# Batch 1's frequency products in three instead of four: a spectral filter with a feed-forward layer on one Trainium2 core

## The chip, the core and the metric

The kernel runs on one core of one Trainium2 chip. A core has TensorE (PE in the profile, its weight loads PEld), VectorE (DVE), ScalarE (ACT), GpSimd (POOL) and SyncE (SP), which issues most DMAs. Each engine takes its own instructions in order. TensorE writes to PSUM, eight banks of 2 KB for each of the 128 partitions; VectorE and ScalarE read PSUM, GpSimd works in SBUF only. The metric is the device time of one execution in microseconds (us).

## What is computed

```python
X = np.fft.rfft(x, axis=1)                      # x: 8 batches, 3008 rows, 256 columns
Yr = Xr @ w_r - Xi @ w_i + b_r
Yi = Xr @ w_i + Xi @ w_r + b_i
Yr = sign(Yr) * max(abs(Yr) - 0.01, 0); the same for Yi
y = np.fft.irfft(Yr + 1j * Yi, n=3008, axis=1)
h = y @ moe_w_in                                # 256 -> 2048
g = where(h > 0, h, exp(min(h, 0)) - 1)
out = g @ moe_w_out                             # 2048 -> 256
```

The kernel does the two Fourier transforms as matrix products in two stages each (3008 = 47 x 64).

## The kernel before, in words

**The main loop** (line 1207) has 47 steps for each batch (`PER`), 376 in all. Step i computes a pair of 128-wide slices of h for a block of 512 rows (`front`, L986, four products 128x512 at L1006 into the tile hps), the exponential on ScalarE (L1022 to L1027), the finish of the step before on VectorE (`finish_elu`, L1048 or L1050, hps and Et to gT), and the second layer's products of step i-2 (`back`, L1080, into ps_o). From step 10 on hps has two buffers, so the hps of step i take the buffer of step i-2, which is free when that step's L1048 or L1050 has run. Every eighth step ends a block, and ps_o is copied out (L1092).

**Between these**, the spectral filter of the next batch is put into the steps as units: A (first transform stage, of the batch after next), X (`unit_X`, L194, its second stage, eight units into the tile XT), M (`unit_M`, L264, the products with the weights, twelve units (q, i), 128 frequencies each), B (`unit_B`, L364, the first inverse stage, six units; B(v) needs both M(v, 0) and M(v, 1)), and Y (`unit_Y`, L530). The function `plan` (L1110) writes out, for each batch, which unit goes into which step: list f0 holds what is issued ahead of `front`, f1 what comes after `finish_elu`. For batch 0's steps, in which batch 1's units run, the order starts at step 10 (`lead = FILL`): X in steps 10 to 17, M(0,0), M(0,1), M(1,0), M(1,1), B(0) in 18 to 22, then M, M, B in turn: B(1) in step 25, B(2) in 28, B(3) in 31, then M(5,0), M(5,1), B(4), B(5) in 32 to 35, and A units and the first Y units from step 36. Steps 0 to 9 hold batch 1's A units and batch 0's last Y units (`split_Y`).

**Who computes the negative branch** changes with the step. In an M step (`on_act`) ScalarE does two passes (L1024, L1025). In steps 0 to 9, and in the later batches' "pool" steps, GpSimd clamps Et (L1059). In the remaining steps that hold a unit, batch 0's X, B and A steps among them, VectorE does it (L1061, one operation of 128x1024 ahead of L1050).

**M units.** A frequency's product of complex X with complex W can be had from four real products (Xr Wr, Xi Wi, Xr Wi, Xi Wr) or from three, with (Xr + Xi) Wr shared and the weight sums Wi + Wr and Wi - Wr. Batches 2 to 7 use three: six products of 128x256 (L289) into two PSUM tiles, of which VectorE copies one (k1) to SBUF (L295, shown as L144) and adds it to the other (L296); GpSimd adds the bias (L301), clips (L302) and subtracts (L303). Their inputs Xr + Xi come from `sum_XT` (L219, GpSimd, L224, six sums of 128x512 a batch, five into XS and one into the tile busy), and the weight sums from `three_weights` (L232, GpSimd, L236, four operations in place on wcat_s, steps 47 to 50). Batches 0 and 1 use four: `m_group` (L240) issues four products of 128x512 (L247), VectorE adds the bias on the way out of PSUM (L257), GpSimd clips and subtracts (L269, L270).

**X units.** Unit u of batches 2 to 7 takes the eight slots of group u % 4 and the half u // 4 of the 256 columns d. Batch 0's and batch 1's take group u // 2 and half u % 2, so that a group of slots is used up before the next. The slots come from the tile Z, which `load_Z` reads back from DRAM; for batch 1 in three parts (slots 0 to 7, 8 to 15, 16 to 31), issued on SyncE's queue in step 5. In step 12 GpSimd runs `gate` (L860), a small copy that waits for Z's third part, ahead of the load of batch 2's first x tile (`load_x`, L117, issued on GpSimd's queue in steps 12, 15 and 18).

Of the kernel before, what the change touches and what calls it, by code (L numbers as in the profile page):

```python
# [8 lines left out]
ALU = mybir.AluOpType  # L9
# [20 lines left out]
def kernel(  # L30
# [11 lines left out]
    nc = tc.nc  # L42
    P = nc.NUM_PARTITIONS

    B, S, D = x.shape
# [5 lines left out]
    LAM = 0.01  # L51
# [42 lines left out]
    PER = S * NPAIR // TB  # L94
# [9 lines left out]
    Y_of = {}  # L104
# [14 lines left out]
    def unit_ps(name, alone):  # L119
        if alone:  # L120
            return pre2.tile([P, 2, 512], F32, name=name, tag="pre2")
        return last_banks("psF").tile([P, 2, 512], F32, name=name, tag="fps")
# [69 lines left out]
        q.dma_start(Z_of[b][r0:r1, s0:s1, :], dv[r0:r1, s0:s1, :])  # L192

    def unit_X(b, u, alone=False, on_dve=False, apart=False):  # L194
        g, dt = (u % 4, u // 4) if b > 1 else (u // 2, u % 2)
        if u == 0:
            XT_of[b] = xtp.tile([P, 2, 2, K1 * N2], BF16, name="XT", tag="XT")
        XT, Z = XT_of[b], Z_of[b]
        if apart:
            psv = [t[:].rearrange("p (k j) -> p k j", j=P) for t in two_banks(pre1, "mps1")]  # L200
        else:
            ps = unit_ps("xps", alone)
            psv = [ps[:].rearrange("p a (k j) -> p (a k) j", j=P)]
        nk = 8 // len(psv)
        for kk in range(8):
            k = 8 * g + kk
            nc.tensor.matmul(  # L207
                psv[kk // nk][:, kk % nk, 0 : 4 * K1], lhsT=Z[:, k, dt * P : dt * P + P],
                rhs=M2[:, k].rearrange("p c m -> p (c m)"), start=True, stop=True,
            )  # L210
        for h, v in enumerate(psv):
            k0 = 8 * g + nk * h
            evac(
                XT[:, dt].rearrange("p c (m s) -> p c m s", s=NS)[:, :, :, k0 : k0 + nk],
                v[:, :, 0 : 4 * K1].rearrange("p k (c m) -> p c m k", c=2),
                bool(h) if apart else on_dve,
            )
# [14 lines left out]
    def three_weights(c, dt):  # L232

        v, r = (w[:, dt, D * c : D * c + D] for w in (wcat_s, wcat_r))
        a, b_ = (r, v) if c else (v, r)
        nc.gpsimd.tensor_tensor(v, a, b_, ALU.subtract)  # L236

    mps_of = {}

    def m_group(b, q, i, ps, biased=False):  # L240
        XT = XT_of[b]
        o = (2 * q + i) * P
        todo = [(c, dt) for c in range(2) for dt in range(2)]
        if b == 0:
            todo.sort(key=lambda z: z[1])
        for c, dt in todo:
            nc.tensor.matmul(  # L247
                ps, lhsT=XT[:, dt, c, o : o + P], rhs=(wcat_r, wcat_s)[c][:, dt, :],
                start=(not biased and (c, dt) == (0, 0)), stop=((c, dt) == (1, 1)),
            )  # L250
        if i == 0:
            Y_of[b, q] = wk3.tile([P, 2, 2 * D], BF16, name="Y", tag="Y")
        if biased:
            yb = ps
        else:
            yb = wk3.tile([P, 2 * D], F32, name="yb", tag="yb")[:]
            nc.vector.tensor_tensor(yb, ps, bias_bc[:], ALU.add)  # L257
        if (b, q, i) == (0, 2, 0):
            clip = late3.tile([P, 2 * D], F32, name="gT", tag="gT")
        else:  # L260
            clip = wk2.tile([P, 2 * D], F32, name="clip", tag="clip")
        return yb, clip

    def unit_M(b, q, i):  # L264
        if b == 1:
            if i == 0:
                mps_of[q] = unit_ps("mps", False)
            yb, clip = m_group(b, q, i, mps_of[q][:, i, :])
            nc.gpsimd.tensor_scalar(clip[:], yb, LAM, -LAM, ALU.min, ALU.max)  # L269
            nc.gpsimd.tensor_tensor(Y_of[b, q][:, i, :], yb, clip[:], ALU.subtract)  # L270
            return
        XT, o = XT_of[b], (2 * q + i) * P
        if i == 0:
            Y_of[b, q] = wk3.tile([P, 2, 2 * D], BF16, name="Y", tag="Y")
        ps, k1 = (
            last_banks("psM").tile([P, 2 * D], F32, name="mps", tag="mps") for _ in range(2)
        )
        ch, oc = divmod(o, 512)
        r, s = wcat_r, wcat_s
        todo = [  # L280
            (k1[:, 0:D], None, r[:, :, 0:D]),
            (ps[:, 0:D], XT[:, :, 1, o : o + P], s[:, :, 0:D]),
            (ps[:, D : 2 * D], XT[:, :, 0, o : o + P], s[:, :, D : 2 * D]),
        ]
        if o == 0 and b > 3:
            todo.append(todo.pop(0))
        for out_, lhs, w in todo:
            for dt in range(2):
                nc.tensor.matmul(  # L289
                    out_, lhsT=lhs[:, dt] if lhs is not None else sum_of(dt, ch)[:, oc : oc + P],  # L290
                    rhs=w[:, dt, :], start=(dt == 0), stop=(dt == 1),
                )
        yb = wk3.tile([P, 2 * D], F32, name="yb", tag="yb")
        clip = wk2.tile([P, 2 * D], F32, name="clip", tag="clip")
        evac(yb[:, D : 2 * D], k1[:, 0:D], True)  # L295
        nc.vector.tensor_tensor(  # L296
            yb[:].rearrange("p (c d) -> p c d", c=2),
            ps[:].rearrange("p (c d) -> p c d", c=2),
            yb[:, D : 2 * D].unsqueeze(1).to_broadcast([P, 2, D]), ALU.add,
        )  # L300
        nc.gpsimd.tensor_tensor(yb[:], yb[:], bias_bc[:], ALU.add)  # L301
        nc.gpsimd.tensor_scalar(clip[:], yb[:], LAM, -LAM, ALU.min, ALU.max)  # L302
        nc.gpsimd.tensor_tensor(Y_of[b, q][:, i, :], yb[:], clip[:], ALU.subtract)  # L303
# [107 lines left out]
    def two_banks(pool, n):  # L411
        return [pool.tile([P, 512], F32, name=n, tag=n) for _ in range(2)]
# [697 lines left out]
    def plan(b):  # L1110

        f0 = [[] for _ in range(PER)]
        f1 = [[] for _ in range(PER)]
        mode = [None] * PER
        n1, n2 = b + 1, b + 2
# [6 lines left out]
        if n1 < B:  # L1122
            if b:
                lead, xs = 0, (3, 6, 9) if b < 3 else (3, 8, 13)
# [28 lines left out]
        else:  # L1153
            lead, seq = 0, [("y", u) for u in range(2, 8)]
# [39 lines left out]
        if n2 < B:  # L1194
            for ci in range(3):
                f1[xs[ci]].append((load_x, (n2, ci)))
        if b and n1 < B:
            f0[seq.index(("X", 4))].append((sum_XT, (n1, 0)))
            f0[seq.index(("X", 7))].append((sum_XT, (n1, 1, range(2 if b < 3 else 3))))
            if b < 3:  # L1200
                f0[seq.index(("M", 2, 0))].insert(0, (sum_XT, (n1, 1, (2,))))
        return f0, f1, mode

    f0 = f1 = None
    bare = 0
    early_h = None
    for i in range(n + LAG):
        if i == FILL:
            few.close()
            psH = ctx.enter_context(  # L1210
                tc.tile_pool(
                    name="psH", bufs=2, space=bass.MemoryType.PSUM, reuse_waits="tile"
                )
            )
        if i == LAG:
            back(0, False)
        if early_h:
            h, on_act = early_h, False
        elif i < n:
            r = i % PER  # L1220
            if r == 0:
                f0, f1, mode = plan(i // PER)
                used = [bool(u0 or u1) for u0, u1 in zip(f0, f1)]
            free = not used[r]
            bare = bare + 1 if free else 0
            calm = free and (i >= n - 2 or (r + 2 < PER and not used[r + 1] and not used[r + 2]))
            for f, a in f0[r]:
                f(*a)
            if mode[r]:
                on_act = mode[r] == "act"  # L1230
                pooled = not on_act
            else:
                on_act = any(f is unit_M for f, a in f0[r])
                pooled = free or i < FILL
            third = calm and bare % 3 == (2 if i // PER == B - 1 else 1)
            h = front(i, third, on_act, pooled)
        finish_elu()
        if i < n:
            for f, a in f1[r]:
                f(*a)  # L1240
            split = i > LAG and (i - LAG) % NPAIR == NPAIR - 1
            if split:
                back(i - LAG, True)
            elu(i, *h, pooled, on_act)
            if PER <= i < PER + 4:
                three_weights(*divmod(i - PER, 2))
            if 1 <= i < 5:
                if i < 3:
                    scale_w_in(2, True, i - 1)
                scale_w_in(3, False, (i - 1) // 2, (i - 1) % 2)  # L1250
            if i == n - 2:
                early_h = front(n - 1, True, False, True)
            elif early_h:
                early_h = None
        else:
            split = False
        if i > LAG and not split:
            back(i - LAG, False)
# [30 lines left out]
```

## Time and profile before

| | |
|---|---|
| device time, median of 3 runs | 894.43 us (894.23 to 895.2) |
| span of the profiled execution | 903.9 us, 18292 instructions |
| TensorE busy | 891.3 us, 99% of the span |
| VectorE, ScalarE, GpSimd busy | 679.6, 722.4 and 596.7 us |
| TensorE's granted clock | 0.948 on average |
| steps 10 to 17 (batch 1's X) | 73.4 to 90.9 us of the span |
| steps 18 to 35 (batch 1's M and B) | 90.9 to 139.0 us |
| GpSimd busy from 90.9 to 136.7 us | 23.22 of 45.8 us |

Times in a trace are us from the start of the span, durations in us or ns. The profile gives no time of the profiled execution other than its span, which is longer than the runs without a profile. In a timeline, matmuls that follow one another overlap, since their ends are modelled: the start of a group is what counts. The chain of work that ended last shows each group only for the time in which nothing before it on the chain was running. Brackets at the end of a timeline's line give how long the engine sat idle before it and what ended that.

### The profile page before, as it was taken

What the parts mean: (1) busy time and instruction counts of PE and PEld (TensorE: products, weight loads), DVE (VectorE), ACT (ScalarE), POOL (GpSimd) and SP (SyncE); (2) the same over time, 40 slices, a digit from 0 to 9 for tenths busy, and PEclk for the clock granted to TensorE, in tenths of its full rate; (3) what the DMA queues carried; (4) which work ended last, traced back from release to release, by engine and by line L of the source; (5) the groups of instructions that cost most, each with busy time, mean ns of one, the idle gap of its engine ahead of it and who ended that gap; (6) DMA issues with size and microseconds to landing.
All of it is one profiled execution on the core that took longest, in us unless ns stands there. A gap on an engine that the chain in (4) does not pass through costs nothing.

```text
span 903.9 us, 18292 instructions
## 1 busy us (share of the span) xinstructions
PE 891.3 (99%) x6917; PEld 675.2 (75%) x6917; DVE 679.6 (75%) x969; ACT 722.4 (80%) x1001; POOL 596.7 (66%) x806
## 2 busy tenths in 40 slices
PE   9999999999999999999999999999999999999997
PEld 3467667877788777877778777787777877777776
DVE  7788778688866887668866788677876678778776
ACT  6778778888978889798887988878887798776654
POOL 7562550788657886588756877559875697753664
PEclk9999999999999999999999999999999999999998
DMA  8996226631474115632265231643218201241111
GB/s 262 310 258 188 70 71 181 169 119 47 118 209 124 65 50 152 173 117 88 72 181 136 86 116 48 189 140 101 87 53 229 70 24 48 69 108 36 28 44 47
DMA packets 90718, 105.85 MB, mean 117 GB/s; under 512 B 5395, under 2 KB 81174, under 8 KB 87302
## 3 DMA queue, kind: packets, MB, share of 16 engines
q1 hardware_dynamic: 84278, 76.64, 30.0%
q0 software_dynamic: 5968, 27.26, 9.4%
q8 instruction: 54, 0.88, 0.4%
q10 hardware_dynamic: 384, 0.79, 0.3%
q14 instruction: 34, 0.28, 0.1%
HBM read 54.86 MB, written 49.81 MB: 116 GB/s over the span
## 4 chain that ended last, share of the span: by engine, by line
PE 90%; DVE 3%; DMA 3%; ACT 2%; POOL 1%; issue 1%; SPq 0%; DVEq 0%; ACTq 0%; POOLq 0%
PE ps_o L1080 37%; PE hps L1006 36%; PE mps L289 5%; PE bps L375 2%; PE xps L207 2%; PE yps L538 2%; PE aps L170 2%; DVE gT L1048 2%; PE mps L247 1%; DVE Bz L144 1%; DMA xt<-in_x_dram 1%; DMA Z<-DA 1%; DMA DB<-Bz 1%; PE sps L1006 1%; DMA DA<-A 0%
## 5 line engine op out<-in xcount | busy, mean ns | idle before, releaser
L1048 DVE SCALAR_TENSOR_TENSOR gT<-Et,hps 128x512 fp32r<-128x512 f32 (+1 forms) x544 | 423.7, 811 | 158.5 <-POOL Et L1059 115.4
L1080 PE MATMUL ps_o<-w_out_r,gT 128*128 128x256 f32 x3008 | 481.4, 303 | 0.0
L1080 PEld LDWEIGHTS ps_o<-w_out_r,gT 128*128 128x128 f32 x3008 | 407.7, 190 | 52.4 <-ACT osb L1092 0.5
L1059 POOL TENSOR_SCALAR Et<-Et 128x512 f32<-128x512 f32 x434 | 258.3, 614 | 223.6 <-ACT Et L1022 213.2
L1006 PE MATMUL hps<-yT,w_in_s 128*128 128x512 bf16 (+7 forms) x1688 | 388.9, 360 | 2.0 <-DVE gT L1048 1.3
L1022 ACT ACTIVATE Et<-hps 128x512 f32<-128x512 f32 x412 | 224.2, 598 | 67.8 <-PE hps L1006 63.3
L1006 PEld LDWEIGHTS <-w_in_s 128*128 128x128 bf16 x1728 | 144.7, 99 | 119.7 <-issue 21.7
L1024 ACT ACTIVATE Et<-hps 128x1024 f32<-128x1024 f32 x130 | 133.6, 1027 | 57.3 <-PE hps L1006 49.0
L1025 ACT ACTIVATE Et<-Et 128x1024 f32<-128x1024 f32 x130 | 137.4, 1057 | 4.1
L301 POOL TENSOR_TENSOR yb<-yb,bias_bc 128x512 f32<-128x512 f32 x72 | 92.3, 1282 | 9.5 <-DVE yb L296 9.4
L303 POOL TENSOR_TENSOR Y<-yb,clip 128x512 bf16<-128x512 f32 x72 | 92.6, 1286 | 6.0
L296 DVE TENSOR_TENSOR yb<-mps,yb 128x512 f32<-128x512 f32 x72 | 49.8, 692 | 7.6 <-PE hps L1006 0.5
L146 ACT CAST XT<-xps 128x768 bf16<-128x768 f32 x57 | 45.5, 799 | 9.8 <-PE xps L207 9.7
L146 ACT CAST A<-aps 128x1024 bf16<-128x1024 f32 x40 | 40.5, 1014 | 11.4 <-PE aps L170 9.9
L302 POOL TENSOR_SCALAR clip<-yb 128x512 f32<-128x512 f32 x72 | 44.2, 614 | 6.3
L289 PE MATMUL mps<-wcat_s,XT 128*128 128x256 bf16 x288 | 44.1, 277 | 0.0
L144 DVE COPY yb<-mps 128x256 f32<-128x256 f32 x72 | 30.3, 421 | 11.1 <-PE mps L289 9.7
L1050 DVE SCALAR_TENSOR_TENSOR gT<-hps,Et 128x1024 fp32r<-128x1024 f32 x29 | 35.5, 1223 | 2.4
L224 POOL TENSOR_TENSOR XS<-XT 128x512 bf16<-128x512 bf16 x30 | 34.1, 1159 | 2.1 <-ACT XT L146 1.2
L1092 DVE COPY osb<-ps_o 128x512 f32<-128x512 f32 x46 | 31.6, 686 | 1.2 <-PE ps_o L1080 0.5
L146 ACT CAST Bz<-bps 128x1024 bf16<-128x1024 f32 x32 | 31.9, 998 | 0.5 <-PE bps L375 0.4
L1027 ACT ACTIVATE Et<-hps 128x1024 f32<-128x1024 f32 x29 | 29.8, 1029 | 2.6 <-PE hps L1006 1.2
(184 smaller groups left out, 678.8 us busy)
## 6 DMA issues: line engine op xcount, KB each, us to landing
xt<-in_x_dram POOLq DMA_DIRECT2D x21, 1024.0 KB, 5.4
out_dram<-osb SPq DMA_DIRECT2D x158, 128.0 KB
Bs<-DB SPq DMA_DIRECT2D x30, 384.0 KB
DB<-Bz SPq DMA_DIRECT2D x20, 512.0 KB
DA<-A SPq DMA_DIRECT2D x19, 512.0 KB
Z<-DA SPq DMA_DIRECT2D x5, 1152.0 KB
Z<-DA SPq DMA_DIRECT2D x11, 384.0 KB
xt<-in_x_dram POOLq DMA_DIRECT2D x6, 512.0 KB, 6.0
```

The lines of the kernel that those rows point to most:

```text
L146: nc.scalar.copy(dst, src)
L289: nc.tensor.matmul(out_, lhsT=lhs[:, dt] if lhs is not None else sum_of(dt, ch)[:, oc : oc + P], rhs=w[:, dt, :], start=(dt == 0), stop=(d ...
L296: nc.vector.tensor_tensor(yb[:].rearrange("p (c d) -> p c d", c=2), ps[:].rearrange("p (c d) -> p c d", c=2), yb[:, D : 2 * D].unsqueeze(1 ...
L301: nc.gpsimd.tensor_tensor(yb[:], yb[:], bias_bc[:], ALU.add)
L303: nc.gpsimd.tensor_tensor(Y_of[b, q][:, i, :], yb[:], clip[:], ALU.subtract)
L1006: nc.tensor.matmul(hps[s][:, c0:c1] if early else hps[:, s, c0:c1], lhsT=w_in_s[:, dt, ft * P : ft * P + P], rhs=yT_of[b][:, dt, t0 : t0 + ...
L1022: nc.scalar.activation(E_[:, s], hps[:, s], AF.Exp)
L1024: nc.scalar.activation(E_, hps[:], AF.Relu, scale=-1.0)
L1025: nc.scalar.activation(E_, E_, AF.Exp, scale=-1.0)
L1048: nc.vector.scalar_tensor_tensor(o, e, -1.0, h, ALU.add, ALU.max)
L1059: nc.gpsimd.tensor_scalar(E_[s], E_[s], 1.0, 0.0, ALU.min, ALU.max)
L1080: nc.tensor.matmul(po[q][:, i_ % 2, :], lhsT=gT[:, s, i_ * P : i_ * P + P], rhs=w_out_r[:, ft, :], start=(ft == 0 and i_ % 2 == 0), stop=( ...
```

## The change

Batch 1's M units lose their own branch and run the code of batches 2 to 7. For this, its X units take the order by halves of d (all four groups for the first half, then all four for the second), `sum_XT` runs on GpSimd after X4's issue in step 14 (first half, three sums) and after X7's in step 17 (second half, three sums), and `three_weights` runs in steps 6 to 9 instead of 47 to 50. M(0,0) of batch 1 issues its product with the sums last of three. Batch 0 keeps four products.

```diff
     def unit_X(b, u, alone=False, on_dve=False, apart=False):
-        g, dt = (u % 4, u // 4) if b > 1 else (u // 2, u % 2)
+        g, dt = (u % 4, u // 4) if b else (u // 2, u % 2)
...
-    mps_of = {}
-
...
     def unit_M(b, q, i):
-        if b == 1:
-            if i == 0:
-                mps_of[q] = unit_ps("mps", False)
-            yb, clip = m_group(b, q, i, mps_of[q][:, i, :])
-            nc.gpsimd.tensor_scalar(clip[:], yb, LAM, -LAM, ALU.min, ALU.max)
-            nc.gpsimd.tensor_tensor(Y_of[b, q][:, i, :], yb, clip[:], ALU.subtract)
-            return
         XT, o = XT_of[b], (2 * q + i) * P
...
-        if o == 0 and b > 3:
+        if o == 0 and (b == 1 or b > 3):
             todo.append(todo.pop(0))
...
-        if b and n1 < B:
+        if b == 0:
+            f0[lead + 4].append((sum_XT, (n1, 0)))
+            f0[lead + 7].append((sum_XT, (n1, 1)))
+        elif n1 < B:
             f0[seq.index(("X", 4))].append((sum_XT, (n1, 0)))
...
-            if PER <= i < PER + 4:
-                three_weights(*divmod(i - PER, 2))
+            if 6 <= i < 10:
+                three_weights(*divmod(i - 6, 2))
```

## Prediction, on record before the result

> **What bounds the kernel now.** I read the page first: engine shares, then the chain of work that ended last.
>
> ```profile
> PE 891.3 (99%) x6917; PEld 675.2 (75%) x6917; DVE 679.6 (75%) x969; ACT 722.4 (80%) x1001; POOL 596.7 (66%) x806
> ...
> PE 90%; DVE 3%; DMA 3%; ACT 2%; POOL 1%; issue 1%; SPq 0%; DVEq 0%; ACTq 0%; POOLq 0%
> ```
>
> TensorE bounds the whole, so a shorter product is worth its full length, unless TensorE then waits. The change acts in two stretches of the timeline: batch 1's X units (steps 10 to 17, from 73.4 us) and its M and B units (steps 18 to 35, 90.9 to 139 us). Next the chain there, and the same work of batch 2 (start, length, what):
>
> ```profile
> 104.54 0.90 PE mps L247 x4
> 105.45 0.90 PE hps L1006 x4
> 106.34 0.94 PE ps_o L1080 x8
> ...
> 187.76 0.68 PE mps L289 x6
> 188.44 0.89 PE hps L1006 x4
> ```
>
> An M step today is 0.90 + 0.90 + 0.94 us with no gap. Batch 2's M unit, which already has three products, takes 0.68 us.
>
> **Gain.** 12 M units x (0.90 - 0.68) = -2.64 us. That is all: it holds only where TensorE does not wait. So I went through what each step of TensorE waits for. hps has two buffers, so the hps products of step i wait until VectorE's L1048/L1050 of step i-2 has read its buffer. The tightest place is a B step followed by two M steps. VectorE's timeline, then TensorE's (start, length):
>
> ```profile
> 105.13 0.70 DVE L1061 TENSOR_SCALAR Et<-Et 128x1024 f32<-128x1024 f32 x1 [0.60 <-ACT Et L1027]
> 105.74 0.69 DVE L257 TENSOR_TENSOR yb<-mps,bias_bc 128x512 f32<-128x512 f32 x1
> 106.34 1.22 DVE L1050 SCALAR_TENSOR_TENSOR gT<-hps,Et 128x1024 fp32r<-128x1024 f32 x1
> ```
> ```profile
> 108.02 1.06 PE L1006 MATMUL hps<-yT,w_in_s 128*128 128x512 bf16 x4
> ```
>
> M(2,0) starts at 104.39. VectorE first finishes step 22's L1061 (it waits for ScalarE's exp, which stands behind two passes of the M step and the eviction L146), then adds the bias for M (L257), then L1050 of step 22, done at 107.56. Step 24's hps start at 108.02: a margin of 0.46 us.
>
> **Cost 1, VectorE's copy (L295).** After the change one more VectorE operation stands in this queue, in front of L1050. Batch 2 shows it:
>
> ```profile
> 188.38 0.41 DVE L144 COPY yb<-mps 128x256 f32<-128x256 f32 x1
> 188.90 0.69 DVE L296 TENSOR_TENSOR yb<-mps,yb 128x512 f32<-128x512 f32 x1
> ```
>
> From copy to add is 0.52 us. L1050 ends 0.52 later, and two shorter M units bring the hps forward by 0.45. So TensorE waits 0.52 + 0.45 - 0.46 = 0.51 us. ScalarE, and with it L1061, keeps its distance to M(2,0), since both hang on the hps two steps earlier. The same sum at the other places (margins from the same two timelines): steps 18/19 margin 0.55, wait 0.42; 26/27, 0.48 and 0.49; 29/30, 0.48 and 0.49; 32/33, 0.49 and 0.48. Five places: +2.39 us. In batch 2 this doesn't occur, because no L1061 runs on VectorE there. I see no reason for less, except that ScalarE's exp came 0.5 us earlier.
>
> **Cost 2, POOL against VectorE.** POOL gets L301 (1.28 us) for each M unit and six sums L224 (1.16 us each); its 1.97 us per unit (L269, L270) become 3.32 (L301 at 189.67 to the next at 192.99). A group of two M and one B step is 7.98 us long (104.39 to 112.36), POOL's part 6.64: it fits, but POOL is then nearly always at work, where it is now idle when L1061 runs. All 29 L1061 take 683 to 697 ns, so that row alone prices a meeting at nothing. But L1061 passes 1024 elements in the time that L257 needs for 512, as L852 does (512 in 0.42), and L852 met POOL early on. VectorE, then POOL:
>
> ```profile
> 42.67 1.01 DVE L852 TENSOR_SCALAR w_in_s<-w_in_f 128x512 bf16<-128x512 f32 x1 [0.40 <-DMA w_in_f<-in_moe_w_in_dram]
> ...
> 52.91 0.42 DVE L852 TENSOR_SCALAR w_in_s<-w_in_f 128x512 bf16<-128x512 f32 x1
> ```
> ```profile
> 42.08 1.32 POOL L332 TENSOR_TENSOR Y<-yb,clip 128x512 bf16<-128x512 f32 x1
> ```
>
> The first ends at 43.68, 0.28 after POOL's operation (43.40). Others end 0.28 after POOL's at 39.05, 42.27 and 54.66. So L1061 will stand until POOL's running operation ends. At a random moment of 3.32 us with pieces of 1.28, 0.61 and 1.28, the rest of a piece is (1.64 + 0.37 + 1.64) / 6.64 = 0.55 us, less some 0.12 of start-up that runs beside it: 0.43. It delays L1050 in front of the same waits, five times: +2.15 us; bounds 0 (POOL between operations) and 5 x 1.14 = 5.7. I take the mean because the phase isn't known.
>
> The Trainium skill, SBUF — State Buffer, Who interferes with whom, says that GpSimd and a VectorE operation in a two-port mode exclude each other for a whole instruction, and that whoever issues first goes first. The four L852 rows agree; by it POOL too would stand behind L1061. By the L1061 row alone the sum below would be 2.55 lower.
>
> **Cost 3, sums in the X steps.** The three sums of the first half (step 14) meet one or two L1061 of X steps. There L1050 ends at 82.31 and the next hps but one starts at 82.51: margin 0.20. A sum of 1.14 leaves 0.57 - 0.14 = 0.43 on average, 0.2 past the margin, twice: +0.4; bounds 0 and 1.6. The second half's first sum starts after X7's eviction (89.27 + 0.80) and ends by 91.3; M(0,0) asks for it last, at 91.4: no wait. L224 in front of load_x delays a load that is used 40 us later: nothing.
>
> **Cost 4, Z earlier.** X2 now reads Z's third part (slots from 16), at step 12 instead of step 14. TensorE's X2 and POOL's gate on that part:
>
> ```profile
> 77.78 0.52 PE L207 MATMUL xps<-M,Z 96*128 96x96 bf16 x8
> ```
> ```profile
> 78.21 0.63 POOL L860 CAST gate<-Z 96x1 f32<-96x1 bf16 x1 [4.81 <-DMA Z<-DA]
> ```
>
> It lands at about 78.2: +0.4 us (bounds 0 and 0.5). X1 reads the second part at 75.59, when about 6 us of transfer since 69.5 have passed for the first half of the bytes: nothing.
>
> **Cost 5, the last B unit.** B(5) needs both M(5) results from POOL. Batch 2's shows the pair's length:
>
> ```profile
> 231.46 1.28 POOL L301 TENSOR_TENSOR yb<-yb,bias_bc 128x512 f32<-128x512 f32 x1 [0.97 <-DVE yb L296]
> ...
> 236.85 1.27 POOL L303 TENSOR_TENSOR Y<-yb,clip 128x512 bf16<-128x512 f32 x1
> ```
>
> 6.66 us. From M(5,0)'s start (128.34 now): L1061 until 1.35 (+0.43), copy 0.52, add 0.69, hand-over 0.1, POOL 6.66: 9.75. TensorE would otherwise reach B(5) at 136.66 - 128.34 = 8.32, less 0.45, plus 0.48 and 0.43 of costs 1 and 2: 8.78. Wait +1.0 us. In batch 2 an A unit stands before B(4), which hides this. B(0) (needed some 10.6 us after M(0,0), POOL done at 9.9 or with the waits both later) and B(1) to B(4): nothing, by a margin that is thin at B(0) only. Steps 35 and 36 lose 0.1 to VectorE's lateness today; after that wait they don't: -0.1.
>
> **Moved to nothing.** The four L236 (0.67 us) go to steps 6 to 9, where POOL sits idle 0.77 and then 1.43 us a step before its clamp L1059; without that cover each would cost TensorE up to 0.67. Out of steps 47 to 50 they free POOL time that TensorE doesn't wait for (its steps there are 2.19 us, without gaps).
>
> **Sum.** -2.64 + 2.39 + 2.15 + 0.4 + 0.4 + 1.0 - 0.1 = +3.6 us. The profiled execution's span is 903.9 us, 1.1% over the runs' median of 894.43; the page gives nothing of what lies around it. The terms are differences inside the span; 1.1% of them is 0.04, so I carry them unscaled: 894.4 + 3.6 = 898.0.
>
> **Rivals.**
> - *No meeting on POOL's side* (costs 2 and 3 vanish): L1061 falls between POOL's operations, or goes first. For it: 29 undisturbed rows. Against it: POOL idle in all of those. 898.0 - 2.55 = 895.5. Chance 0.2.
> - *Faster*: every M unit's 0.22 us is kept, because exp and L1061 come at least 0.5 us earlier beside M (ScalarE catching up while it has less to wait for), so L1050 is in time in spite of the copy, and POOL ends M(5) in time for the same reason. Decides at a margin of 0.97 us in front of hps instead of 0.46. Then -2.64 + 0.4 = 892.2. Against it: ScalarE's two passes start from the hps that shift along. Chance 0.12.
> - *POOL becomes the bound*: every meeting costs nearly a whole operation and POOL, held in turn, delays each B unit. Cost 2 at 5.7, cost 3 at 1.6: 898.0 + 3.55 + 1.2 = 902.8. POOL's 6.64 in 8 us speaks against a lasting queue. Chance 0.08.
> - That the change doesn't do what it says can be excluded nearly: the products follow from the code.
>
> **Numbers.** The forecast has 0.6 and spans 896.4 to 900. The range reaches to the no-meeting case: 894.9 to 900.2; left out are the faster case and most of the last. A measurement here can tell about 0.2% (1.8 us) from no change: faster (below 892.6) 0.10, same (to 896.2) 0.27, slower 0.63.
>
> **What would show it.** In the changed profile: L289 with 72 more products, TensorE's M groups 0.68; VectorE L1050 as releaser of hps in steps 19, 24, 27, 30, 33, with gaps of 0.4 to 1 us; L1061 longer than 0.7 us where POOL runs L301 to L303; X2 near 78.2; B(5) released by POOL L303. If L1061 stays at 0.69 and hps start without gaps, costs 1 and 2 were wrong; if steps 6 to 9 lengthen, the four L236 were not free.

## The result and the profile after

The changed kernel takes 898.94 us (median of 4 runs, 897.96 to 899.59), the one before 894.33 us (4 runs beside them, 893.64 to 895.2): a ratio of 1.005, 95% interval 1.0036 to 1.0065. It is slower by some 4.6 us, and by 4.0 us in a second series (e13 below). The forecast of 898.0 us came within 1 us, with the right sign. The terms behind it were partly wrong in size.

The page of the changed kernel, the lines that answer to those shown of before:

```profile
span 896.2 us, 18380 instructions
...
PE 877.4 (98%) x6941; PEld 671.1 (75%) x6941; DVE 688.8 (77%) x981; ACT 722.6 (81%) x1001; POOL 620.2 (69%) x824
...
PE 86%; DVE 6%; ACT 3%; issue 2%; DMA 2%; POOL 1%; SPq 0%; DVEq 0%; ACTq 0%; POOLq 0%
```

The two profiles can't be subtracted. The first one of before was taken at a granted clock of 0.948 (span 903.9 us), that of after at 1.000. What follows compares profiles at 0.998 to 1.000, unless it names the first profile, and so begins with a new profile of the kernel before (e1). Its line of the chain is:

```profile
PE 89%; DVE 5%; ACT 2%; issue 2%; POOL 1%; DMA 1%; DVEq 0%; ACTq 0%; POOLq 0%
```

So at full clock TensorE's share of the chain falls from 89% to 86%, and VectorE's rises from 5% to 6%; the 90% and 3% shown for before are those of the first profile, at the lower clock. That is a hint that TensorE waits for VectorE in more places; where it does, the timelines show.

From the M code on, after's line numbers are 9 lower: the clamp L1061 is L1052, L1048/L1050 are L1039/L1041, hps L1006 is L997, the three products L289 are L280, and POOL's L301 to L303 are L292 to L294.

### The profile page after: what moved, and what is told of

It is laid out like the page before. It is cut to its first block, busy times and chain, and to the rows that moved or that the text cites. A ratio compares the mean times of both kernels' runs of the same rounds, so it can differ in the third digit from the quotient of the medians.

```text
span 896.2 us, 18380 instructions
## 1 busy us (share of the span) xinstructions
PE 877.4 (98%) x6941; PEld 671.1 (75%) x6941; DVE 688.8 (77%) x981; ACT 722.6 (81%) x1001; POOL 620.2 (69%) x824
## 4 chain that ended last, share of the span: by engine, by line
PE 86%; DVE 6%; ACT 3%; issue 2%; DMA 2%; POOL 1%; SPq 0%; DVEq 0%; ACTq 0%; POOLq 0%
PE ps_o L1071 35%; PE hps L997 34%; PE mps L280 6%; PE bps L366 2%; PE xps L207 2%; PE yps L529 2%; DVE gT L1039 2%; PE aps L170 2%; DVE Bz L144 1%; DVE gT L1041 1%; DMA Z<-DA 1%; PE sps L997 1%; DMA xt<-in_x_dram 0%; DVE A L144 0%; ACT Et L1018 0%
## 5 line engine op out<-in xcount | busy, mean ns | idle before, releaser
L1039 DVE SCALAR_TENSOR_TENSOR gT<-Et,hps 128x512 fp32r<-128x512 f32 (+1 forms) x544 | 423.8, 811 | 153.2 <-POOL Et L1050 111.8
L1071 PE MATMUL ps_o<-w_out_r,gT 128*128 128x256 f32 x3008 | 476.5, 301 | 0.1
L1050 POOL TENSOR_SCALAR Et<-Et 128x512 f32<-128x512 f32 x434 | 258.4, 614 | 213.6 <-ACT Et L1013 205.4
L997 PE MATMUL hps<-yT,w_in_s 128*128 128x512 bf16 (+7 forms) x1688 | 377.9, 351 | 5.9 <-DVE gT L1041 2.9
L997 PEld LDWEIGHTS <-w_in_s 128*128 128x128 bf16 x1728 | 142.9, 98 | 119.4 <-issue 25.6
L292 POOL TENSOR_TENSOR yb<-yb,bias_bc 128x512 f32<-128x512 f32 x84 | 107.7, 1282 | 14.1 <-DVE yb L287 12.6
L294 POOL TENSOR_TENSOR Y<-yb,clip 128x512 bf16<-128x512 f32 x84 | 108.0, 1286 | 7.0
L287 DVE TENSOR_TENSOR yb<-mps,yb 128x512 f32<-128x512 f32 x84 | 58.1, 692 | 8.8 <-DVE yb L144 0.5
L293 POOL TENSOR_SCALAR clip<-yb 128x512 f32<-128x512 f32 x84 | 51.9, 617 | 7.4
L280 PE MATMUL mps<-wcat_s,XT 128*128 128x256 bf16 x336 | 50.5, 273 | 1.4 <-DVE yb L287 1.1
L224 POOL TENSOR_TENSOR XS<-XT 128x512 bf16<-128x512 bf16 x35 | 40.2, 1171 | 9.1 <-ACT XT L146 8.2
L144 DVE COPY yb<-mps 128x256 f32<-128x256 f32 x84 | 35.3, 420 | 9.9 <-PE mps L280 9.2
L1041 DVE SCALAR_TENSOR_TENSOR gT<-hps,Et 128x1024 fp32r<-128x1024 f32 x29 | 35.5, 1223 | 2.4
L280 PEld LDWEIGHTS <-XT 128*128 128x128 bf16 x336 | 32.4, 98 | 6.1 <-issue 1.8
```

The source lines that it names most:

```text
L280: nc.tensor.matmul(out_, lhsT=lhs[:, dt] if lhs is not None else sum_of(dt, ch)[:, oc : oc + P], rhs=w[:, dt, :], start=(dt == 0), stop=(d ...
L287: nc.vector.tensor_tensor(yb[:].rearrange("p (c d) -> p c d", c=2), ps[:].rearrange("p (c d) -> p c d", c=2), yb[:, D : 2 * D].unsqueeze(1 ...
L997: nc.tensor.matmul(hps[s][:, c0:c1] if early else hps[:, s, c0:c1], lhsT=w_in_s[:, dt, ft * P : ft * P + P], rhs=yT_of[b][:, dt, t0 : t0 + ...
L1039: nc.vector.scalar_tensor_tensor(o, e, -1.0, h, ALU.add, ALU.max)
L1050: nc.gpsimd.tensor_scalar(E_[s], E_[s], 1.0, 0.0, ALU.min, ALU.max)
L1071: nc.tensor.matmul(po[q][:, i_ % 2, :], lhsT=gT[:, s, i_ * P : i_ * P + P], rhs=w_out_r[:, ft, :], start=(ft == 0 and i_ % 2 == 0), stop=( ...
```

## The experiments

**What is measured.** The stretch in which the change acts runs from batch 1's first X unit to batch 2's first X unit. In each trace that is the distance between two starts of TensorE, which leaves out what comes ahead (the first X unit starts at 71.0 to 73.4 us, whatever the kernel; what sets that was not tried). All ratios are to runs of the kernel before on the same chip, with 95% intervals.

| run | what it is | median us | ratio | stretch us |
|---|---|---|---|---|
| e1 | before, profile at clock 0.999 | 894.32 | one run | 92.45 |
| after | the change | 898.94 | 1.005 (1.0036 to 1.0065) | 97.12 |
| e13 | the change again | 898.01 | 1.0043 (1.0029 to 1.0057) | 97.09 |
| e2 | no bias add on POOL | 895.11 | 1.0013 (1.0003 to 1.0022) | 94.28 |
| e3 | k1's copy on ScalarE | 897.38 | 1.0035 (1.0022 to 1.0048) | 94.45 |
| e4 | A(0) ahead of B(4) | 899.29 | 1.0055 (1.004 to 1.007) | 97.75 |
| e5 | before, with the X part alone | 894.79 | 1.0009 (1.0 to 1.0019) | 93.27 |
| e8 | clamps of B steps off VectorE | 892.93 | 0.9984 (0.9974 to 0.9994) | 91.96 |
| e9 | e8, bias on VectorE | 893.9 | 0.9999 (0.9989 to 1.0008) | 92.56 |
| e10 | e9, X clamps on POOL | 893.4 | 0.999 (0.9981 to 1.0) | 92.03 |
| e11 | e10, bias on POOL again | 892.46 | 0.998 (0.9971 to 0.999) | 91.51 |
| e12 | e11, bias on VectorE for M(5,·) alone | 891.59 | 0.997 (0.9958 to 0.9981) | 91.06 |

**e1: the kernel before, once more.** No edit.

> The kernel before, unchanged, for a second profile: the first one was taken at a granted clock of 0.948, the changed kernel's at 1.0, so stretches of the two cannot be subtracted. Both theories: 894.3 us; from M(0,0) to the first A unit some 47.5 us (48.14 in the first profile), and no gap in front of hps in steps 19, 24, 27, 30 and 33. If such gaps are there already, the change did not make them.

Its timeline has the two starts of TensorE that bound the stretch, 163.62 - 71.17 = 92.45 us apart (start, length, engine, line):

```profile
71.17 0.50 PE L207 MATMUL xps<-M,Z 96*128 96x96 bf16 x8 [0.17 <-DVE yT L144]
...
163.62 0.52 PE L207 MATMUL xps<-M,Z 96*128 96x96 bf16 x8
```

The same two in the changed kernel, 97.12 us apart:

```profile
71.76 0.50 PE L207 MATMUL xps<-M,Z 96*128 96x96 bf16 x8 [0.17 <-DVE yT L144]
...
168.88 0.52 PE L207 MATMUL xps<-M,Z 96*128 96x96 bf16 x8
```

So the stretch holds +4.67 us, as much as the whole loss (the later batches give some 0.6 us back, see the end). Where in it? Busy time by window: the columns are window, its length, busy us (instructions) of PE, PEld, DVE, ACT and POOL, granted clock, DMA share, GB/s. First the kernel before (e1), X steps and then M steps:

```profile
71.20:88.40 17.20, 17.04 (x158) 13.84 (x162) 14.89 (x17) 14.78 (x17) 1.73 (x3) 1.00 0.55 173
88.40:135.40 47.00, 46.50 (x307) 31.62 (x313) 34.18 (x40) 37.33 (x40) 23.27 (x25) 1.00 0.28 82
```

Then the changed kernel:

```profile
71.20:88.40 17.20, 16.74 (x157) 13.12 (x155) 14.87 (x17) 14.03 (x17) 6.52 (x8) 1.00 0.64 197
88.40:135.40 47.00, 42.81 (x314) 31.93 (x312) 39.69 (x49) 33.66 (x36) 39.36 (x38) 1.00 0.23 68
```

Both kernels are cut at the same times, though the M steps of after run from 89.44 to 140.84, so its second window begins a little early and leaves out the end. In the M steps TensorE was idle for 0.5 of 47 us, and is now idle for 4.2. POOL goes from 23.27 to 39.36 us and VectorE from 34.18 to 39.69, neither of them full. One place shows how they act together: a B step followed by two M steps. VectorE before (e1):

```profile
102.29 0.69 DVE L1061 TENSOR_SCALAR Et<-Et 128x1024 f32<-128x1024 f32 x1 [0.61 <-ACT Et L1027]
102.90 0.68 DVE L257 TENSOR_TENSOR yb<-mps,bias_bc 128x512 f32<-128x512 f32 x1
103.50 1.22 DVE L1050 SCALAR_TENSOR_TENSOR gT<-hps,Et 128x1024 fp32r<-128x1024 f32 x1
```

It is done at 104.72, and TensorE's hps (e1) start without a gap at 105.03:

```profile
105.03 1.03 PE L1006 MATMUL hps<-yT,w_in_s 128*128 128x512 bf16 x4
```

The same place after the change, VectorE:

```profile
103.78 1.29 DVE L1052 TENSOR_SCALAR Et<-Et 128x1024 f32<-128x1024 f32 x1 [0.61 <-ACT Et L1018]
104.99 0.41 DVE L144 COPY yb<-mps 128x256 f32<-128x256 f32 x1
105.50 0.69 DVE L287 TENSOR_TENSOR yb<-mps,yb 128x512 f32<-128x512 f32 x1
106.11 1.22 DVE L1041 SCALAR_TENSOR_TENSOR gT<-hps,Et 128x1024 fp32r<-128x1024 f32 x1
```

POOL there:

```profile
103.24 1.27 POOL L292 TENSOR_TENSOR yb<-yb,bias_bc 128x512 f32<-128x512 f32 x1
104.60 0.94 POOL L293 TENSOR_SCALAR clip<-yb 128x512 f32<-128x512 f32 x1
```

And TensorE:

```profile
105.47 0.39 PE L280 MATMUL mps<-wcat_r,XS 128*128 128x256 bf16 x2
106.25 0.60 PE L280 MATMUL mps<-wcat_s,XT 128*128 128x256 bf16 x4 [0.38 <-DVE yb L287]
107.38 1.02 PE L997 MATMUL hps<-yT,w_in_s 128*128 128x512 bf16 x4 [0.53 <-DVE gT L1041]
```

The clamp takes 1.29 us instead of 0.69 and ends at 105.07, 0.56 after POOL's L292 (104.51). The copy adds its slot. L1041 ends at 107.33, and TensorE has waited twice: 0.38 for the PSUM tile of the M unit before, which the add L287 empties, and 0.53 for hps. (These idle times are too short, because the ends of matmuls are modelled; starts are safer.) From the M unit's start to hps it is 1.91 us, where it is 0.67 without waits (102.99 to 103.66): 1.24 us lost. Both waits are one delay, since hps could not start before the end of L1041. The five places lose 1.19, 1.24, 1.26, 1.00 and 1.00, together 5.69 us. The experiments take this sum apart.

**e2: no bias add on POOL.** It leaves out the bias of batch 1, so that its results lack it; POOL's part per M unit falls from 3.32 to about 2 us.

```diff
-        nc.gpsimd.tensor_tensor(yb[:], yb[:], bias_bc[:], ALU.add)
+        if b != 1:
+            nc.gpsimd.tensor_tensor(yb[:], yb[:], bias_bc[:], ALU.add)
```

> GpSimd's bias add L292 is left out for batch 1 (its part of the output lacks the bias), so GpSimd works 3.9 us a pair of M units instead of 6.6 and should be idle when VectorE's clamp L1052 (L1061 before) runs in the B steps. Theory (VectorE's queue in front of hps: the copy, and the clamp standing behind GpSimd): the clamps of steps 22, 25, 28 and 31 return from 1.29, 1.62, 1.03 and 1.05 to 0.69 us, which is 2.2 us, and the wait of B(5) for GpSimd, 1.0 us, goes: 898.9 - 3.2 = 895.7. Rival (only the copy delays hps; the longer clamp costs nothing): only B(5)'s wait goes: 897.9. Gaps of about 0.5 us in front of hps remain under both.

VectorE's clamps in two of the B steps of e2, whose line L1053 is L1052 of after:

```profile
104.74 0.69 DVE L1053 TENSOR_SCALAR Et<-Et 128x1024 f32<-128x1024 f32 x1 [0.61 <-ACT Et L1019]
...
112.78 0.69 DVE L1053 TENSOR_SCALAR Et<-Et 128x1024 f32<-128x1024 f32 x1
```

The four clamps of the B steps are back at 0.69 us; that of step 17, which meets a sum L224, still takes 1.40. At these four places 0.64, 0.50, 0.65 and 0.62 us of wait are left: the price of VectorE's copy without POOL, 0.60 on average. With 1.19 less its clamp's 0.70 at step 19, the copy costs 4 x 0.60 + 0.49 = 2.9 us, and POOL's meeting the other 5.69 - 2.9 = 2.8. The stretch gets 2.84 us shorter, most of it here (0.60 + 0.92 + 0.33 us from M(2,0) to M(5,0)) and 1.10 from M(5,0) to A(0), where B(5)'s wait goes too. The time, 895.11, fits the first theory (895.7) and not the rival (897.9).

**e3: k1's copy on ScalarE.** One argument of `evac` chooses the engine:

```diff
-        evac(yb[:, D : 2 * D], k1[:, 0:D], True)
+        evac(yb[:, D : 2 * D], k1[:, 0:D], b != 1)
```

> Batch 1's copy of k1 (L286) is done by ScalarE, which is idle 0.34 us or more in each M step. Theory (VectorE's queue in front of hps): VectorE's 0.52 us from copy to add goes at five places: 898.9 - 2.6 = 896.3; the clamps stay long, and B(5) still waits for GpSimd. Rival (GpSimd's 6.6 us a pair sets the pace of the M and B steps): the copy is not what is waited for, at most 0.5 us less: 898.4.

The stretch falls by 2.67 us, close to the 2.6 expected. The median, 897.38, lies between the two theories, and its six runs spread from 895.93 to 899.16; in the profiled one the first X unit started at 73.38, 2.2 us later than in e1, outside of what was edited. By its time the run is inconclusive. In its trace the five places lose 2.84 us instead of 5.69. That is near the 2.9 that e2 gives for the copy, but not a clean measure of it: the clamps, too, meet GpSimd at other moments (longer by 2.41 us together, in after by 2.93), and step 21 has a new wait of 0.40.

**e4: an A unit ahead of B(4),** to hide B(5)'s wait as batch 2 does:

```diff
-                    [u for u in mid if u[0] != "A"]
-                    + [("A", 0), ("A", 1), ("A", 2), ("n", 0), ("n", 1)]
+                    [u for u in mid if u[0] != "A"][:24]
+                    + [("A", 0), ("B", 4), ("B", 5), ("A", 1), ("A", 2), ("n", 0), ("n", 1)]
```

> The first A unit moves from behind B(5) to in front of B(4), as batch 2 has it, so GpSimd gets a step more for M(5). Theory: B(5)'s wait of 1.0 us goes, and nothing else: 897.9. Rival (the wait only moves: B(5), its store and its load back come a step later, the first Y unit of batch 1 waits for them): 898.9 or more.

TensorE at B(5) and at the first Y unit in e4:

```profile
140.84 0.61 PE L366 MATMUL bps<-Y,M 64*128 64x256 bf16 x8
...
148.94 0.49 PE L529 MATMUL yps<-M,Bs 96*128 96x94 bf16 x8 [1.02 <-DMA Bs<-DB]
```

B(5) runs in one piece without a wait, but the Y unit now waits 1.02 us for Bs, which must be written out and read back after B(5). The wait only moved, as the rival had it; the stretch is 0.63 us longer.

**e5: the X part alone,** the kernel before with the order by halves and the sums in steps 14 and 17, but four products:

```diff
-        g, dt = (u % 4, u // 4) if b > 1 else (u // 2, u % 2)
+        g, dt = (u % 4, u // 4) if b else (u // 2, u % 2)
...
-        if b and n1 < B:
+        if b == 0:
+            f0[lead + 4].append((sum_XT, (n1, 0)))
+            f0[lead + 7].append((sum_XT, (n1, 1)))
+        elif n1 < B:
```

> The kernel before with only the X part of the change: batch 1's X units by halves of d, and the six sums on GpSimd, whose results nothing reads; M keeps four products and the weight sums stay in steps 47 to 50. Theory: the first half's sums hold one clamp of an X step for half a microsecond (0.46 us in front of hps in the changed kernel), the second half's the clamp of step 17, which costs little here (margin 0.55 us, no copy); Z lands in time: 894.3 + 0.6 = 894.9. Rival (the early need of Z, or the sums themselves, make a large part of the 4.6 us): 896 or more.

VectorE's clamps of steps 14 and 17:

```profile
82.79 1.24 DVE L1061 TENSOR_SCALAR Et<-Et 128x1024 f32<-128x1024 f32 x1
...
90.06 1.40 DVE L1061 TENSOR_SCALAR Et<-Et 128x1024 f32<-128x1024 f32 x1
```

POOL's sums alone, in a kernel without the new products, lengthen L1061 from 0.69 to 1.24 and 1.40 us. The stretch grows by 0.82 us and TensorE waits 0.46 in the X steps, 0.27 in step 19; the median of 894.79 is what was expected (894.9).

**e8: no clamp on VectorE in the B steps and the last X step.** There ScalarE takes the two passes of an M step, and VectorE the unit's eviction in ScalarE's place.

```diff
+            elif b == 0 and u in [("X", 7)] + [("B", v) for v in range(4)]:
+                f0[t].append(put(u[0], n1, u[1], False, *((True,) if u[0] == "X" else (False, True))))
...
-                on_act = any(f is unit_M for f, a in f0[r])
+                on_act = any(
+                    f is unit_M or (f is unit_X and a[1] == 7) or (f is unit_B and a[1] < 4)
+                    for f, a in f0[r]
+                ) and i < PER
```

> The changed kernel, with the clamp taken off VectorE in the five steps ahead of an M unit (X7's and B(0) to B(3)'s): ScalarE does two passes there as in M steps, and VectorE takes X7's eviction and half of each B's. GpSimd has the same work as in the changed kernel. Theory (VectorE's queue in front of hps): without a clamp nothing stands behind GpSimd and the copy fits, so the waits of M steps, 5.7 us in the changed kernel's trace, go; B(5) still waits for GpSimd: 898.9 - 5.7 = 893.2, if ScalarE, with some 7 us of work in a group of 7.4, keeps up. Rival (GpSimd's pair of M units sets the pace): GpSimd is as busy as before, 897.5 or more.

The expectation has VectorE take half of each B's eviction; in the run it took all of it (128x1024, 1.22 us). The same place as above, TensorE:

```profile
104.58 0.39 PE L280 MATMUL mps<-wcat_r,XS 128*128 128x256 bf16 x2
104.81 0.60 PE L280 MATMUL mps<-wcat_s,XT 128*128 128x256 bf16 x4
105.25 1.03 PE L997 MATMUL hps<-yT,w_in_s 128*128 128x512 bf16 x4
```

From M to hps 0.67 us, no wait. At four of the five places at most 0.06 us is left; at step 27, where the copy of ps_o (L1083) stands in VectorE's queue, 0.24 (M to hps takes 0.91). The kernel is faster than before by 0.16% (0.06 to 0.26), and its stretch is 0.49 us shorter. So most of what the change lost comes back once VectorE's queue has no clamp ahead of the copy. What is left besides are 0.55 us at B(5), 0.54 at the product with the sums in step 18 and 0.45 in the X steps.

**e9: e8 with k1 and the bias added in one operation on VectorE,** in place of the copy and of POOL's add:

```diff
-        evac(yb[:, D : 2 * D], k1[:, 0:D], True)
+        if b == 1:
+            nc.vector.tensor_tensor(
+                yb[:].rearrange("p (c d) -> p c d", c=2),
+                bias_bc[:].rearrange("p (c d) -> p c d", c=2),
+                k1[:, 0:D].unsqueeze(1).to_broadcast([P, 2, D]), ALU.add,
+            )
+        else:
+            evac(yb[:, D : 2 * D], k1[:, 0:D], True)
```

> The kernel without the five clamps, and batch 1's bias is added by VectorE in the operation that takes k1 out of PSUM (128x512 instead of 128x256, 0.69 instead of 0.42 us), so GpSimd has two operations a unit instead of three. Theory: B(5)'s wait for GpSimd goes as well, 0.9 us: 892.3, below the kernel before. Rival (VectorE or ScalarE is full in the groups of M, M, B): 893.2 or more.

VectorE in e9 (lines are numbered anew: L287 is the new operation, L294 the add that is L287 in after):

```profile
105.63 0.68 DVE L287 TENSOR_TENSOR yb<-bias_bc,mps 128x512 f32<-128x512 f32 x1
106.78 0.69 DVE L294 TENSOR_TENSOR yb<-mps,yb 128x512 f32<-128x512 f32 x1 [0.47 <-DVE yb L287]
107.38 1.21 DVE L1048 SCALAR_TENSOR_TENSOR gT<-Et,hps 128x1024 fp32r<-128x1024 f32 x1
```

The rival was right: with 0.68 us in place of the copy's 0.41 VectorE is late again, and TensorE waits 0.34 to 0.44 us in steps 19, 25 and 27. B(5)'s wait is gone, but in all it is 1 us slower than e8.

**e10, e11 and e12: the rest of the waits.** e10 is e9 with the clamps of batch 1's X steps on POOL, and ScalarE's two passes in the steps of X4 and X7, where the sums run:

```diff
-                    f is unit_M or (f is unit_X and a[1] == 7) or (f is unit_B and a[1] < 4)
+                    f is unit_M or (f is unit_X and a[1] in (4, 7)) or (f is unit_B and a[1] < 4)
...
-                pooled = free or i < FILL
+                pooled = free or i < FILL or not on_act and i < PER and any(
+                    f is unit_X for f, a in f0[r]
+                )
```

e11 is e10 without e9's edit: the copy is back, and the bias is on POOL. e12 is e11 with e9's edit for the last pair alone (shown against e9):

```diff
-        if b == 1:
+        if (b, q) == (1, 5):
```

> As the last, and X0 to X6 have their clamp on GpSimd, X4 two passes on ScalarE, as batches 2 to 7 have it, so no clamp runs on VectorE while GpSimd makes the sums. Theory: the 0.46 us of the X steps goes too: 891.8. Rival (ScalarE with X4's two passes, or GpSimd with sums and clamps, is late in the X steps): 892.3 or more.

> No clamp on VectorE in steps 10 to 17 nor in the B steps ahead of an M unit, the bias back on GpSimd (as in the kernel with five clamps away, whose trace still has 0.45 us in front of hps in the X steps, 0.5 us in step 18 in front of the product with the sums, and 0.55 us in front of B(5)). Theory: the first two go, less 0.2 for X4's and X6's steps: 892.9 - 0.8 = 892.1. Rival (GpSimd, now with the X steps' clamps, enters the M steps late and B(0) waits): 892.9 or more.

> As the last, and for M(5,0) and M(5,1) alone VectorE adds the bias while it takes k1 out of PSUM, so that GpSimd is done with them 2.6 us sooner. Theory: B(5)'s 0.5 us goes: 891.6. Rival (VectorE's longer operation delays hps in step 33 by as much): 892.1.

e10 gives 893.4 us, on its rival's side (892.3 or more), and half a us better than e9. e11 gives 892.46, midway between its theory (892.1) and the rival (892.9), and so decides nothing by its time; its stretch is 0.45 us shorter than e8's. e12 gives 891.59 (891.6 expected). TensorE at B(5) in e12 starts without a wait:

```profile
131.47 0.61 PE L375 MATMUL bps<-Y,M 64*128 64x256 bf16 x8
132.01 1.04 PE L1006 MATMUL hps<-yT,w_in_s 128*128 128x512 bf16 x4
```

At 0.997 (0.9958 to 0.9981) of the kernel before, e12 beats both kernels, by 2.4 us and by about 6.4 us (e13 is on its chip). 1.39 of the 2.4 us lie in the stretch. Moving the clamps alone, with four products, was not tried; but in e1 TensorE is idle for only 0.81 us of the stretch, so that could hardly have given the 1.39.

**e13: the change again** on that chip, without an edit.

> The changed kernel, unchanged, on the same chip as these: 898.9 us. In the profiles so far the stretch from batch 1's first X unit to batch 2's is 97.1 us against 92.5 before, 4.7 longer, and the time before it differs between runs (71.2 to 73.4 us). If the change costs time only in that stretch, this profile has 97.1 us there again, give or take 0.2, whatever the whole run takes.

Its stretch is 97.09 us, and its lengthened clamps are 1.42, 1.34, 1.64, 1.04 and 1.04 us, where after has 1.39, 1.29, 1.62, 1.03 and 1.05.

## Why the prediction was right, step by step

The stretch's +4.67 us, from the starts in the two traces (after less e1), beside the terms on record:

| step | predicted | measured |
|---|---|---|
| gain, 12 M units | -2.64 | 12 x (0.665 - 0.875) = -2.52 |
| cost 1, VectorE's copy | +2.39 | +2.9 |
| cost 2, clamp behind POOL | +2.15 | +2.8 |
| cost 3, sums in the X steps | +0.4 | +0.5 |
| cost 4, Z earlier | +0.4 | 0 |
| cost 5 and steps 35, 36 | +0.9 | +0.5 |
| L236 in steps 6 to 9 | 0 | 0 |

That sums to +4.2 against 4.67: 0.17 stands at B(1)'s hps and 0.15 at M(3,1)'s start, where no wait is recorded, and the rest is rounding. That the forecast's +3.6 came so close to the +4.0 to +4.6 of the two series was partly luck. The errors were opposite: two costs too small by 1.2 us together, two too large by 0.8. And some 0.6 us come back in later batches, which the forecast did not have.

- **Cost 1** was right in mechanism and place: VectorE releases hps in steps 19, 24, 27, 30 and 33, each time. The term that was mis-sized is the margin. 0.46 us was read from a profile at clock 0.948, in which TensorE takes longer and VectorE doesn't; at clock 1.0 it is 105.03 - 104.72 = 0.31. With the measured gain of 2 x 0.21, the same sum gives 0.52 + 0.42 - 0.31 = 0.63 a place; e2 measured 0.60.
- **Cost 2** was right too, and with it the place given to the L852 rows over the 29 undisturbed L1061. The mean over a random phase was not: the phase repeats, and after and e13 have the same five lengths to 0.05 us. The five are longer by 2.93 us together, instead of 2.15. (For the start-up that runs beside the wait the prediction took 0.12 us here and 0.14 in cost 3; the lengthened clamps end 0.55 us after GpSimd's operation, which gives 0.69 - 0.55 = 0.14.) The rival without a meeting needed 0.69 at every one of them. It is out in after and e5, and holds in e2's B steps, where POOL has no bias add.
- The Trainium skill, SBUF — State Buffer, Who interferes with whom, says that GpSimd and a VectorE operation in a two-port mode exclude each other for a whole instruction, and that whoever issues first goes first. The rows agree in both directions: the clamp stood behind POOL's L292, and POOL's clip L293, next in line, took 0.94 us instead of 0.61.
- Of VectorE's operations in the M steps only the clamp is held up. From 89 to 140 us of after, beside the same GpSimd work, two of its lines have (busy us, mean ns | idle before):

```profile
L287 DVE TENSOR_TENSOR yb<-mps,yb 128x512 f32<-128x512 f32 x12 | 8.3, 692 | 1.6 <-DVE yb L144 0.5
L1052 DVE TENSOR_SCALAR Et<-Et 128x1024 f32<-128x1024 f32 x6 | 7.1, 1180 | 2.9 <-ACT Et L1018 2.9
```

The add L287 keeps the 0.69 us that it has alone, and so do the copy (0.41) and L1041 (1.22).
- **Cost 3**: step 14's clamp is 1.24 us long and hps of step 16 waits; VectorE, then TensorE in after:

```profile
82.89 1.24 DVE L1052 TENSOR_SCALAR Et<-Et 128x1024 f32<-128x1024 f32 x1
```
```profile
85.51 1.02 PE L997 MATMUL hps<-yT,w_in_s 128*128 128x512 bf16 x4 [0.29 <-DVE gT L1041]
```

- **Cost 4** failed. It took the landing of Z's third part from one profile, the first, in which POOL's gate on it starts at 78.21, 4.79 us after the first X unit. X2 asks for it some 4.3 us after that unit. After the change X2 starts at 76.09 without a recorded wait, and the gate at 76.10:

```profile
76.09 0.51 PE L207 MATMUL xps<-M,Z 96*128 96x96 bf16 x8
```
```profile
76.10 0.18 POOL L851 CAST gate<-Z 96x1 f32<-96x1 bf16 x1 [3.74 <-DMA Z<-DA]
```

There the data came just in time, 4.34 us after the first X unit; in e1 it is 3.41, in e13 3.50 and in e8 2.81. So the landing keeps no fixed distance to the X units, and of the profiles in which the gate waits for it the first has the latest one. Whether an execution like the first would have made X2 wait, no run shows. (The gate's length there, 0.63 us instead of 0.18, is another thing: it lay beside an L1061 from 78.11 to 78.80.)

- **Cost 5**: the pair's length was right (9.75 us predicted from M(5,0)'s start to POOL's end, 128.99 to 138.67 = 9.68), and so was TensorE's arrival (8.78 predicted, 8.76 measured). What was missed is that B(5) has two halves, and only the second needs M(5,1). TensorE in after, then POOL:

```profile
137.75 0.39 PE L366 MATMUL bps<-Y,M 64*128 64x256 bf16 x4 [0.17 <-ACT Bz L146]
138.71 0.39 PE L366 MATMUL bps<-Y,M 64*128 64x256 bf16 x4 [0.57 <-POOL Y L294]
```
```profile
137.40 1.27 POOL L294 TENSOR_TENSOR Y<-yb,clip 128x512 bf16<-128x512 f32 x1
```

The first four products run 0.96 us ahead of the others, so that 0.57 us of wait is left of the 1.0. B(4)'s start to A(0)'s grows by 0.70 us, and 0.16 comes back after it.
- **Moved to nothing** was right: from the ps_o products of step 6 to those of steps 7, 8, 9 and 10 it is 2.66, 2.62, 2.62 and 2.38 us in after, and 2.65, 2.62, 2.62 and 2.37 in e1.
- **The faster rival** wanted a margin of 0.97 us in front of hps; at full clock it was 0.31. e8 shows what it hoped for in another kernel: there VectorE is in time in spite of the copy, but because the clamp is gone, not because it came earlier.

What stays open: the cycles of the later batches are together some 0.6 us shorter in the kernels with the whole change (538.40 us against 539.02), and not in e5, which keeps the weight sums in steps 47 to 50. With it, e4, e8 to e12 and e13 come to within 0.4 us of the time that their stretch gives, after and e2 to 0.5; e3 is 1.7 us slower than that. Moving the weight sums alone was not tried, and they can hardly be all of it: 0.33 of the 0.6 us is one wait of TensorE's hps for VectorE at 513.39 us in e1 (0.30 at 514.67 in e5), which the kernels with the whole change don't have, and e1's weight sums are over by 170 us. Why the wait is gone there stays open.

## What to carry to other kernels

Cheaper products on the bound engine are only worth something if the engines that finish them have room in the same steps: list what they gain (here a copy on VectorE and a longer chain on GpSimd), and look for the places where the bound engine waits for a buffer with a margin below that. Read such margins from a profile at full granted clock. Where GpSimd becomes busy, look in the trace for the VectorE operations that grow longer beside it (here the in-place clamp, and not the adds), and take them out of the tight queue (e8) before the new work goes in.

## What was not expected of the hardware

- With TensorE's granted clock at 0.948 instead of 1.0, TensorE's groups are longer (a four-product M unit 0.90 instead of 0.875 us) and VectorE's and POOL's operations are not (L1050 1.22 us in both, L257 0.69 and 0.68, POOL's L270 1.27 and 1.28): the margin between TensorE and VectorE is another one (0.46 and 0.31 us).
- The meeting of VectorE's clamp and GpSimd costs both: a clamp of 0.69 us takes 1.03 to 1.64 beside operations of 1.28, a clip of 0.61 takes 0.94.
